# Keeping the sums of w_in from block 1 in HBM, in a retention and quick-GELU kernel

## The chip, the cores and the metric

The kernel runs on one core of a Trainium2 chip. The metric is device time in microseconds (us). Before the change, three runs gave a median of 659.03 us (656.14, 659.03 and 660.89).

The engines are named as in the profile: PE is TensorE's matrix multiply and PEld its weight load, DVE is VectorE, ACT is ScalarE, POOL is GpSimd, SP is SyncE. ACT, POOL and SP can each issue DMAs from a queue of their own; "ACTq" or "SPq" is such an instruction in that engine's stream.

## The reference

A recurrent retention layer over 4 batches, 8 heads, 768 steps and head size 64 gives x (3072 tokens by 512). Behind it stands a two-layer network with w_in (512 by 2048) and w_out (2048 by 512):

```python
state = gamma[None, :, None, None] * state + np.einsum('bhd,bhe->bhde', k[:, :, t], v[:, :, t])
y[:, :, t] = scale * np.einsum('bhd,bhde->bhe', q[:, :, t], state)
...
h = x @ w_in
g = h * (1.0 / (1.0 + np.exp(-1.702 * h)))
return (g @ w_out).astype(np.float32)
```

All is float32; the kernel is handed the two weight matrices as 64-bit numbers and narrows them itself.

## The kernel before

The 3072 tokens are worked through in six blocks of 512 (two halves of 256). Retention is done in steps of 64 positions; its step j is `step`, `attend`, `masked`, `by_state`, `output`, `aged` and `updated`. A block's *first product* is x @ w_in with the gate, its *second product* is g @ w_out.

**The sums.** From block 1 on, the first product is done with seven products of half-size matrices instead of eight. A 512 by 256 piece of w_in (two of the eight column groups p, so four pieces d = 0 to 3) is held as four quarters w0 to w3 in W1A. The seven products need four sums of them: w4 = w2 + w3, w5 = w4 - w0, w6 = w0 - w2, and w1 - w5. Block 0 needs no sums; its first product (`up0`, PE line 417) reads w0 to w3 as they are.

**Where the sums were made.** Twice:

- For block 1's first product (`seven`, PE line 492; sums in `seven_4`, `seven_6`, `seven_52`, `seven_w`, `seven_v`) into tiles of their own, one set for each d in the order 2, 0, 1, 3. Set 2 is made by DVE (lines 449, 453, 458, 459). In the other three, DVE makes w4, ACT writes a negated quarter (lines 465 and 474), and POOL issues a DMA from SBUF to SBUF that adds the other quarter to it (lines 467 and 475). The fourth sum, called w2, had a tile of its own, in the slot kT or tmp.
- Once more, for blocks 2 to 5, by POOL in `sums_w1` (lines 522 to 527), during block 1's second product: three sums into W1L, a view of the tile LATE, and the fourth in place over w2 in W1A.

LATE (48 rows of 128 numbers in each partition, 3 MB in all) has other uses too. Block 0 keeps gated results in it until its second product is over. From block 2 on, parts of it hold what `stream` and `derive` need for the second product. So in block 2, behind the first and the second `up`, SP stored LATE's two halves to the HBM tiles W1D[0] and W1D[1] (line 1003), and blocks 3 to 5 load them back (line 766 by ACT, line 999 by POOL).

**What sets the order.** Up to the end of block 1's first product, the order of the work is written out by hand as a list of words (lines 959 to 977); each word is a function that issues its instructions, and `pin` keeps each engine's order as written. `abs9` is ACT's first step of narrowing a piece of weights, `half9` and `rest9` are DVE's; `w9a` and `w9b` are SP's loads of the raw piece; `q7`, `v7` are loads for a retention step; `gate0.1.3` is ACT's gate for `up0.1.3`; `seven2.4` is the fifth of the seven products for d = 2. Behind the list PE still goes in program order; the other engines' instructions are placed by a scheduler where they are not kept in order. An engine works through its stream in order, so a DMA that waits on ACT holds what is behind it on ACT.

Between the products of `seven`, ACT copies the running sum out of PSUM (`p1`, `u` and `vv`, line 497) before PE may go on adding to that bank, one product later.

Before, the calls around the change in the loop over the blocks m were:

```python
pool.dma_start(LATE[:, 0:24], W1D[0])                                        # line 999, m > 2
tc.keep_in_program_order(sp.dma_start(W1D[n], LATE[:, 24 * n:24 * n + 24]))  # line 1003, m == 2, n < 2
if m == 1 and n % 8 == 3:
    sums_w1(n // 4)                                                          # line 1020
```

Of the kernel before, what the change touches and what calls it, by code (L numbers as in the profile page):

```python
# [9 lines left out]
F32 = mybir.dt.float32  # L10
U32 = mybir.dt.uint32
AF = mybir.ActivationFunctionType
ALU = mybir.AluOpType
P = 128
# [14 lines left out]
def kernel(  # L29
# [29 lines left out]
    pe, act, dve, pool, sp = nc.tensor, nc.scalar, nc.vector, nc.gpsimd, nc.sync  # L59
# [19 lines left out]
    one = ctx.enter_context(tc.tile_pool(name="one", bufs=1))  # L79
    two = ctx.enter_context(tc.tile_pool(name="two", bufs=2))  # L80
# [9 lines left out]
    W1A = const.tile([P, NP, 4, 2, P], F32, name="W1A")  # L90
    LATE = late.tile([P, 2 * NP * 3, P], F32, name="LATE")
    W1L = LATE.rearrange("p (n s c) f -> p n s c f", s=3, c=2)
    W1D = [dram.tile([P, NP * 3, P], F32, name=f"W1D{i}") for i in range(2)]
# [20 lines left out]
    def w1(p, s):  # L114

        return W1A[:, p, s] if s < 4 else W1L[:, p, s - 4]

    def w1s(p):

        return [W1A[:, p:p + 2, s] for s in range(4)] + [W1L[:, p:p + 2, s] for s in range(3)]  # L120

    ordered = [True]

    def pin(i):
        return tc.keep_in_program_order(i) if ordered[0] else i
# [142 lines left out]
    def decay(j):  # L268

        if j % NC == NC - 1:  # L270
            return
        KD[j] = home(j, "kd")
        x = QKV["kn", j]
        if j < NEW:

            for h in range(H):
                pin(act.activation(KD[j][:, h], x[:, h % HP * 2 + h // HP], AF.Copy, scale=cold[:, H + h:H + h + 1]))
        else:
            pin(pool.tensor_mul(KD[j].rearrange("p (i s) d -> p i s d", i=2), x.rearrange("p (i s) d -> p i s d", i=2),
                                cold[:, None, H:H + HP, None].to_broadcast([P, 2, HP, D])))  # L280
# [152 lines left out]
    SUM_X, SUM_W = {}, {}  # L433
# [20 lines left out]

    def seven_52(d):
        m = SUM_W[d]
        m.append(one.tile([P, 2, 2 * P], F32, name="w2", tag="kT"))
        pin(dve.tensor_sub(m[5], m[4], m[0]))
        pin(dve.tensor_sub(m[7], m[1], m[5]))

    def seven_w(d):

# [6 lines left out]
    def seven_v(d):  # L469

        m = SUM_W[d]
        m.append(one.tile([P, 2, 2 * P], F32, name="w2", tag="kT") if d == 1 else
                 two.tile([P, 2, 2 * P], F32, name="w2", tag="tmp", bufs=1))
        pin(act.activation(m[7], m[5], AF.Copy, scale=-1.0))
        pin(pool.dma_start(m[7], m[1], accum_op=ALU.add))

    SEVEN, GATES = {}, []

# [4 lines left out]
    def seven(d, k):  # L483
# [34 lines left out]
            pin(dve.tensor_add(a[2], acc, SEVEN["t"]))  # L518
        else:
            GATES.append(((a[3], a[3]), (a[2], a[2]), (a[1], acc)))  # L520

    def sums_w1(p):
        w = w1s(p)
        pool.tensor_add(w[4], w[2], w[3])
        pool.tensor_sub(w[6], w[0], w[2])
        pool.tensor_sub(w[5], w[4], w[0])
        pool.tensor_sub(w[2], w[1], w[5])

    def sums_x():
        tc.keep_in_program_order(pool.tensor_sub(X[:, 4], X[:, 2], X[:, 0]))  # L530
# [10 lines left out]
    def sums_w2_t3(p):  # L541
        dve.tensor_sub(W2[:, 6, p:p + 2, :], W2[:, 5, p:p + 2, :], W2[:, 0, p:p + 2, :])
# [92 lines left out]
    def inner_w2_t3(i):  # L635

        b11, b12, b21, b22 = w2q(ORDER[i][1])
        tc.keep_in_program_order(dve.tensor_sub(b12, b22, b12))
# [12 lines left out]
    def stream(i, engine=pool):  # L651

        c = LATE[:, i % 2 * 24:i % 2 * 24 + 12].rearrange("p (k d) e -> p k d e", k=3)
        engine.dma_start(c, W2D[i])  # L654
        return c
# [273 lines left out]
    works |= {"seven_x": seven_x, "seven_end": seven_end}  # L929
    for d in range(NP // 2):  # L930
        works |= {f"seven_{n}.{d}": lambda d=d, do=do: do(d)
                  for n, do in (("4", seven_4), ("6", seven_6), ("52", seven_52), ("w", seven_w), ("v", seven_v))}
        for n in range(7):
            works[f"seven{d}.{n}"] = lambda d=d, n=n: seven(d, n)
    for i in range(2 * NFF):
        works[f"w{i // 2}{'ab'[i % 2]}"] = lambda i=i: fetch(i)
    for name, i in [("0a", 0), ("0b", 1)] + [(str(p), 2 * p) for p in range(1, NFF)]:
        n = Narrow(i)
# [20 lines left out]
    for name in """  # L959
        k0 table q0 warm turn0 w0b rows warm k1 abs0b q1 turned0 step0 v0 w0a half0b mask k2 turn1 causal rest0b  # L960
        masked0 decay0 v1 decay1 abs0a half0a step-0 updated0 turned1 q2 step1 rowd whole w2b turn2 w2a x0 k3
        aged1 masked1 turned2 v2 rest0a abs2 q3 step-1 updated1 state1 decay2 aged2 step2 q4 x1 half2 decay3 w3b
        w3a up0.0.0 masked2 turn3 k4 step-2 v3 q5 rest2 k5 gate0.0.0 turned3 updated2 state2 step3 up0.0.2
        masked3 abs3 half3 x2 rest3 turn4 w1b step-3 aged3 gate0.0.2 turned4 state3 w1a w5b updated3 v5 decay4
        abs1 x3 turn5 half1 up0.0.3 turned5 up0.1.2 step4 aged4 w5a rest1 v4 gate0.0.3 decay5 w6a masked4
        gate0.1.2 abs5 w6b step5-4 half5 rest5 up0.0.1 updated4 abs6 state4 gate0.0.1 w4b
        up0.1.1 half6 aged5 w4a up0.0.5 rest6 masked5 up0.1.5 gate0.1.1 x4 gate0.0.5 abs4 step-5 w8b w8a
        half4 gate0.1.5 state5 updated5 anew q6 up0.1.6 x5 rest4 gate0.1.6 abs8 v6 decay6 aged6 up0.0.6 w7b w7a half8
        turn6 gate0.0.6 up0.1.0 abs7 seven_4.2 seven_6.2 half7 gate0.1.0 w9b w9a up0.1.4 q7 gate0.1.4 step6 masked6 rest7 up0.0.4 v7
        gate0.0.4 seven_52.2 turn7 up0.1.3 gate0.1.3 step7-6 seven_4.0 masked7 updated6 decay7 aged7 abs9 state6 x6 up0.0.7 rest8 seven_w.0 gate0.0.7  # L970
        w11a w11b step-7 state7 x7 seven_x half9 w10b w10a up0.1.7 gate0.1.7
        seven2.0 seven2.1 abs11 rest9 seven2.2 seven_v.0 w12a w12b seven2.3 half11 seven2.4 abs10 seven_4.1 seven_w.1
        seven2.5 rest11 seven2.6 w14b w14a seven0.0 seven0.1 half10 seven0.2 abs12 seven0.3 rest10 w13a w13b seven0.4
        seven_v.1 seven0.5 seven_4.3 half12 seven_w.3 seven0.6 seven1.0 abs14 seven1.1 rest12 w15a w15b seven1.2 seven1.3
        half14 seven1.4 abs13 seven_v.3 seven1.5 updated7 rest14 seven1.6 seven3.0 seven3.1 half13 seven3.2 abs15 seven3.3
        rest13 seven3.4 seven3.5 late_loads half15 rest15 seven3.6 seven_end
    """.split():
        works[name]()
    ordered[0] = False
    INNER = [(0, 19), (0, 22), (0, 26), (1, 2), (1, 12), (1, 15), (1, 18)]  # L980
    for m in range(NB):
        between = []
        if m == 0:
            between = [lambda: None, lambda: None, lambda: turn(2 * CB), lambda: step(2 * CB), lambda: None,
                       lambda: turn(2 * CB + 1)]
        elif m == 1:
            between = [lambda: (decay(2 * CB), load(2 * CB + 1, "v"))]
            for j in range(2 * CB + 1, 3 * CB + 1):
                between.append(lambda j=j: (step(j, j - 1), j < 3 * CB and turn(j + 1)))
        elif 1 < m < NB - 1:  # L990
            last = min((m + 2) * CB, NCH - 1)
            for j in range((m + 1) * CB + 1, last + 1):
                between.append(lambda j=j: (step(j, j - 1), j < last and turn(j + 1)))
            if last == NCH - 1:
                between.append(lambda: step(None, NCH - 1))
        if m > 1:
            ds = (0, 1, 2, 3) if m == 2 else (2, 3, 0, 1)
            if m > 2:
                pool.dma_start(LATE[:, 0:24], W1D[0])
            for n, d in enumerate(ds):  # L1000
                up(d, ds[n - 1] if n else None, ds[n + 1] if n < 3 else None)
                if m == 2 and n < 2:
                    tc.keep_in_program_order(sp.dma_start(W1D[n], LATE[:, 24 * n:24 * n + 24]))
                if n == 0 and m < NB - 1:
                    turn((m + 1) * CB + 1)
                if d == 0:
                    comps = {0: stream(0)}
                if n == 2:
                    comps[1] = stream(1)
                if m == 2:  # L1010
                    for i in range(2 * d, min(7, 2 * d + 2)):
                        inner_w2_t3(i)
        for n, unit in enumerate(down(m) if m < 2 else down49(m, comps)):
            unit()
            if m == 0 and n < NP and n % 2:
                sums_w2(n - 1)
            if m == 0 and NP <= n < 3 * NP // 2:
                sums_w2_t3(2 * (n - NP))
            if m == 1 and n % 8 == 3:
                sums_w1(n // 4)  # L1020
            if (m, n) in INNER:
                inner_w2(INNER.index((m, n)))
            if between and (n in (2, 5, 11, 16, 21) if m == 1 else n % 3 == (1 if m else 2)):
                between.pop(0)()
            if 0 < m < NB - 1 and n == (23 if m == 1 else 11):
                sums_x()
# [46 lines left out]
```

## Time and profile before

The profiled execution spans 659.4 us from its first to its last instruction; the profile gives no other time for it, and its span lies between the timed runs. PE's granted clock over the span was 0.995 of full speed.

| stage | us from the start | what happens |
|---|---|---|
| loading, first steps | 0 to 44 | PE busy 32.0 us, DMA engines full |
| block 0's first product, retention steps 4 to 7 | 44 to 103.3 | PE busy 58.1 us |
| block 1's first product with the sums | 103.3 to 151.7 | ACT busy 24.7 us |
| second products of blocks 0 and 1 | 151.7 to 259.5 | POOL busy 50.8 us |
| block 2 | 259.5 to about 364 | SP's two stores to W1D at 267.2 and 286.2 |
| blocks 3, 4, 5 | 364 to 659.4 | W1D loaded back three times |

Other rows that the change touches:

| what | number |
|---|---|
| DMA traffic in all | 89.77 MB |
| LATE<-W1D, 1536 KB each | by ACT's queue 3 times, 7.6 us to landing; by POOL's 3 times, 7.8 us |
| SP's two issues of W1D<-LATE | 0.40 and 0.60 us, 7.3 to 8.5 us to landing with all transfers of W1D |
| ACT's negations, L465 (6) and L474 (3) | about 0.62 us each |

A busy time is a sum over instructions; a gap on an engine matters only if PE, which is busy 97% of the span, ends up waiting for it. A wait is put down to what came last.

### The profile page before, as it was taken

What the parts mean: (1) busy time and instruction counts of PE and PEld (TensorE: products, weight loads), DVE (VectorE), ACT (ScalarE), POOL (GpSimd) and SP (SyncE); (2) the same over time, 40 slices, a digit from 0 to 9 for tenths busy, and PEclk for the clock granted to TensorE, in tenths of its full rate; (3) what the DMA queues carried; (4) which work ended last, traced back from release to release, by engine and by line L of the source; (5) the groups of instructions that cost most, each with busy time, mean ns of one, the idle gap of its engine ahead of it and who ended that gap; (6) DMA issues with size and microseconds to landing.
All of it is one profiled execution on the core that took longest, in us unless ns stands there. A gap on an engine that the chain in (4) does not pass through costs nothing.

```text
span 659.4 us, 15196 instructions
## 1 busy us (share of the span) xinstructions
PE 639.5 (97%) x6390; PEld 577.1 (88%) x6390; DVE 427.4 (65%) x599; ACT 165.2 (25%) x320; POOL 195.7 (30%) x222
## 2 busy tenths in 40 slices
PE   6789999999999999999999999999999999999997
PEld 3678888888788888889999888999888999888997
DVE  3699989999936963348883336984145984144855
ACT  4674334551000000333101323100333210233210
POOL 6400321210478218000727400535500335500000
PEclk9799999999999999999999999999999999999999
DMA  9996649763243456550577821486741244601142
GB/s 174 185 274 186 175 89 246 188 139 54 48 96 144 120 155 160 183 169 1 157 161 213 224 50 49 124 192 175 235 79 49 71 141 145 237 2 49 52 157 97
DMA packets 148149, 89.77 MB, mean 136 GB/s; under 512 B 131600, under 2 KB 134416, under 8 KB 147056
## 3 DMA queue, kind: packets, MB, share of 16 engines
q1 hardware_dynamic: 135856, 44.66, 30.2%
q0 software_dynamic: 9456, 38.16, 18.5%
q10 hardware_dynamic: 2768, 5.96, 2.6%
q8 instruction: 50, 0.82, 0.5%
q14 instruction: 19, 0.16, 0.1%
HBM read 71.32 MB, written 14.94 MB: 131 GB/s over the span
## 4 chain that ended last, share of the span: by engine, by line
PE 83%; DMA 8%; DVE 4%; SPq 2%; POOL 1%; issue 1%; ACT 0%; DVEq 0%; ACTq 0%; POOLq 0%
PE pq L679 22%; PE px L564 16%; PE pd L814 13%; PE pz L564 8%; PE ph L417 8%; PE ph L492 7%; PE py L564 4%; DMA W<-in_moe_w_in_dram 2%; PE pa L294 2%; DMA LATE<-W1D 1%; DMA G<-in_moe_w_in_dram 1%; PE py L317 1%; PE py L311 1%; PE pa L302 1%; DMA kn_in<-in_k_dram 1%; SPq L146 1%
## 5 line engine op out<-in xcount | busy, mean ns | idle before, releaser
L654 POOL DMA_DIRECT2D LATE<-W2D x28 | 15.5, 555 | 236.4 <-PE pq L679 125.0
L679 PE MATMUL pq<-W,G 128*128 128x128 f32 x672 | 80.2, 276 | 0.0
L679 PEld LDWEIGHTS pq<-W,G 128*128 128x128 f32 x672 | 77.6, 192 | 0.6
L564 PE MATMUL px<-X,LATE 128*128 128x256 f32 x256 | 60.7, 380 | 2.2 <-DMA LATE<-W1D 1.2
L564 PE MATMUL px<-X,W1A 128*128 128x256 f32 x256 | 60.5, 379 | 0.0
L679 PE MATMUL pq<-LATE 128*128 128x128 f32 x448 | 59.8, 276 | 0.0
L417 PE MATMUL ph<-X,W1A 128*128 128x256 f32 x256 | 57.4, 382 | 1.6 <-DVE X L352 1.1
L564 PEld LDWEIGHTS px<-X,LATE 128*128 128x128 f32 x256 | 48.5, 190 | 9.5 <-issue 1.5
L417 PEld LDWEIGHTS ph<-X,W1A 128*128 128x128 f32 x256 | 48.0, 190 | 8.5 <-DVE X L352 1.2
L679 PEld LDWEIGHTS pq<-LATE 128*128 128x128 f32 x448 | 54.5, 192 | 0.4
L564 PEld LDWEIGHTS px<-X,W1A 128*128 128x128 f32 x256 | 48.4, 190 | 6.5
L814 PE MATMUL pd<-W,G 128*128 128x256 f32 x224 | 49.6, 381 | 0.0
L814 PEld LDWEIGHTS pd<-W,G 128*128 128x128 f32 x224 | 42.2, 190 | 5.8
L599 DVE TENSOR_TENSOR G<-pz,vv 128x512 f32<-128x512 f32 x16 | 11.1, 692 | 49.3 <-ACT vv L579 49.3
L398 ACT ACTIVATE G<-G 128x512 f32<-128x512 f32 x48 | 29.8, 628 | 44.4 <-DVE G L607 22.2
L814 PE MATMUL pd<-W,LATE 128*128 128x256 f32 x160 | 35.8, 382 | 1.2 <-DVE LATE L548 1.2
L814 PEld LDWEIGHTS pd<-W,LATE 128*128 128x128 f32 x160 | 30.1, 190 | 6.2 <-DVE LATE L548 2.2
L701 ACT ACTIVATE o<-pq 128x512 f32<-128x512 f32 (+1 forms) x14 | 7.6, 544 | 90.8 <-PE pq L679 90.8
L564 PE MATMUL pz<-X,W1A 128*128 128x256 f32 x128 | 30.3, 379 | 0.0
L564 PE MATMUL py<-X,W1A 128*128 128x256 f32 x128 | 30.2, 379 | 0.0
L564 PE MATMUL pz<-X,LATE 128*128 128x256 f32 x128 | 30.2, 379 | 0.0
L679 PE MATMUL pq<-LATE,G 128*128 128x128 f32 x224 | 29.6, 275 | 0.0
(206 smaller groups left out, 1175.3 us busy)
## 6 DMA issues: line engine op xcount, KB each, us to landing
LATE<-W2D POOLq DMA_DIRECT2D x28, 768.0 KB, 5.0
W<-in_moe_w_in_dram SPq DMA_DIRECT2D x12, 512.0 KB, 4.8
W<-in_moe_w_out_dram SPq DMA_DIRECT2D x10, 512.0 KB, 5.0
out_dram<-o POOLq DMA_DIRECT2D x20, 256.0 KB, 3.8
q_sq<-in_q_dram SPq DMA_DIRECT2D x144, 32.0 KB, 2.5
k_sq<-in_k_dram SPq DMA_DIRECT2D x144, 32.0 KB, 2.2
v_in<-in_v_dram SPq DMA_DIRECT2D x72, 64.0 KB, 3.0
LATE<-W1D ACTq DMA_DIRECT2D x3, 1536.0 KB, 7.6
```

Source lines behind the costliest of these rows:

```text
L146: keep(engine.dma_start(*((to, at) if name == "v" else (to[:, n:H:2], at[:, n * HP:(n + 1) * HP]))))
L294: pe.matmul(pa[HALF[w], u, 0, s, :], kt[HALF[u], w, s, :], qt[HALF[u], w, s, :], start=True, stop=True)
L302: pe.matmul(pa[HALF[u], w, 1, s, :], kd[HALF[w], HP * u + s, :], vn[HALF[w], HP * u + s, :], start=True, stop=True)
L398: pin(act.activation(g, h[:, i], AF.Gelu_apprx_sigmoid))
L417: pe.matmul(h[:, ab], w, X[:, 2 * th + c // 2, c % 2, :], start=(ab == 0 and c == 0), stop=(c == 3), skip_group_check=True)
L492: pe.matmul(acc[:, u, :], w, x, start=(start and u == 0 and c == 0), stop=(stop and c == 1), skip_group_check=True)
L564: pe.matmul(acc[:, u, :], w1(2 * d + u, sw)[:, c, :], X[:, sx, c, :], start=(start and u == 0 and c == 0), stop=(stop and c == 1), skip_gr ...
L599: dve.tensor_add(a[3], z, v)
L654: engine.dma_start(c, W2D[i])
L679: pe.matmul(p0[:, j, :], a[:, d], w[:, d], start=(new and j == 0 and d == 0), stop=(d == NP // 2 - 1), skip_group_check=True)
L701: act.activation(to, y, AF.Copy)
L814: pe.matmul(p0[:, n, :], g1(m, p, sa)[:, n * P:(n + 1) * P], W2[:, sb, p, :], start=(new and p == 0 and n == 0), stop=(last and p == NP - ...
```

## The change

The sums made for block 1's first product are no longer thrown away.

- The fourth sum is written in place over w2 in W1A (by DVE in set 2, by ACT and POOL's adding DMA in the others) and has no tile of its own any more.
- The other three of a set are stored to W1D by three DMAs on ACT's queue (`seven_out`), for sets 0, 1 and 3 right behind `seven_v`, for set 2 behind `step7-6` in the list. Each store moves 256 KB in rows of 1 KB.
- POOL's `sums_w1` and the helper `w1s` are gone.
- At the start of block 1's second product ACT's queue loads LATE's two halves from W1D; SP's two stores in block 2 are gone.

```diff
     def seven_52(d):
         m = SUM_W[d]
-        m.append(one.tile([P, 2, 2 * P], F32, name="w2", tag="kT"))
+        m.append(m[2])
         pin(dve.tensor_sub(m[5], m[4], m[0]))
-        pin(dve.tensor_sub(m[7], m[1], m[5]))
+        pin(dve.tensor_sub(m[2], m[1], m[5]))
...
     def seven_v(d):
 
         m = SUM_W[d]
-        m.append(one.tile([P, 2, 2 * P], F32, name="w2", tag="kT") if d == 1 else
-                 two.tile([P, 2, 2 * P], F32, name="w2", tag="tmp", bufs=1))
-        pin(act.activation(m[7], m[5], AF.Copy, scale=-1.0))
-        pin(pool.dma_start(m[7], m[1], accum_op=ALU.add))
+        m.append(m[2])
+        pin(act.activation(m[2], m[5], AF.Copy, scale=-1.0))
+        pin(pool.dma_start(m[2], m[1], accum_op=ALU.add))
+        seven_out(d)
+
+    def seven_out(d):
+
+        to = W1D[d // 2].rearrange("p (n s c) f -> p n s (c f)", s=3, c=2)[:, d % 2 * 2:d % 2 * 2 + 2]
+        for n in range(3):
+            pin(act.dma_start(to[:, :, n], SUM_W[d][4 + n]))
...
-    def sums_w1(p):
-        w = w1s(p)
-        pool.tensor_add(w[4], w[2], w[3])
-        pool.tensor_sub(w[6], w[0], w[2])
-        pool.tensor_sub(w[5], w[4], w[0])
-        pool.tensor_sub(w[2], w[1], w[5])
...
-        gate0.0.4 seven_52.2 turn7 up0.1.3 gate0.1.3 step7-6 seven_4.0 masked7 updated6 decay7 aged7 abs9 state6 x6 up0.0.7 rest8 seven_w.0 gate0.0.7
+        gate0.0.4 seven_52.2 turn7 up0.1.3 gate0.1.3 step7-6 seven_out.2 seven_4.0 masked7 updated6 decay7 aged7 abs9 state6 x6 up0.0.7 rest8 seven_w.0 gate0.0.7
...
         elif m == 1:
+            for n in range(2):
+                act.dma_start(LATE[:, 24 * n:24 * n + 24], W1D[n])
             between = [lambda: (decay(2 * CB), load(2 * CB + 1, "v"))]
...
-                if m == 2 and n < 2:
-                    tc.keep_in_program_order(sp.dma_start(W1D[n], LATE[:, 24 * n:24 * n + 24]))
...
-            if m == 1 and n % 8 == 3:
-                sums_w1(n // 4)
```

More of the change, by code (lines that the diff above doesn't have):

```diff
@@ L116, in w1 @@
         return W1A[:, p, s] if s < 4 else W1L[:, p, s - 4]
-    def w1s(p):
-        return [W1A[:, p:p + 2, s] for s in range(4)] + [W1L[:, p:p + 2, s] for s in range(3)]
     ordered = [True]
@@ L931 @@
         works |= {f"seven_{n}.{d}": lambda d=d, do=do: do(d)
-                  for n, do in (("4", seven_4), ("6", seven_6), ("52", seven_52), ("w", seven_w), ("v", seven_v))}
+                  for n, do in (("out", seven_out), ("4", seven_4), ("6", seven_6), ("52", seven_52), ("w", seven_w), ("v", seven_v))}
         for n in range(7):
```

## The prediction

> **What bounds the kernel now.** I read the page's busy shares first, then PE's waits from 44 us to the end, then the busy time by stage, then single engines around the edits.
>
> ```profile
> PE 639.5 (97%) x6390; PEld 577.1 (88%) x6390; DVE 427.4 (65%) x599; ACT 165.2 (25%) x320; POOL 195.7 (30%) x222
> ```
>
> PE works 639.5 of 659.4 us. The 19.9 us without PE are 12.0 in the first 44 us (loading), 3.9 in the last 48 and little between. PE's waits from 44 us on (line, who was waited for, total us, times, longest):
>
> ```profile
> PE pd L814 <- DVE LATE L548: 1.2, 2, 0.9
> PE px L564 <- DMA LATE<-W1D: 1.2, 1, 1.2
> PE px L564 <- POOL X L532: 1.0, 1, 1.0
> PE pa L294 <- DVE G L323: 0.9, 1, 0.9
> PE ph L417 <- DVE W1A L227: 0.5, 1, 0.5
> ```
>
> Stages (window, length, busy us of PE, PEld, DVE, ACT, POOL, then clock, DMA share, GB/s):
>
> ```profile
> 103.30:151.70 48.40, 48.40 (x226) 42.61 (x225) 46.40 (x56) 24.66 (x41) 9.29 (x8) 1.00 0.73 183
> 165.00:180.00 15.00, 13.83 (x92) 11.07 (x90) 15.00 (x22) 0.00 (x0) 6.16 (x5) 1.00 0.28 53
> 180.00:213.00 33.00, 33.00 (x156) 28.79 (x156) 15.91 (x15) 1.79 (x3) 27.00 (x21) 1.00 0.37 112
> ```
>
> 103 to 152 is block 1's first product, where the sums are made: PE has no gap, DVE 2.0 us in 48.4. At 165 to 180 DVE is full and PE loses 1.2. At 180 to 213 POOL makes its second set, and PE has no gap. PE's idle time over all middle stages is 1.25 + 1.17 + 0.54 + 0.49 + 1.04 + 0.12 = 4.6 us. The change adds and removes no matmul and touches neither the first 44 us nor the tail. So 4.6 us (0.7%) is the most that it can give.
>
> **POOL's second set, removed.** Four sums, four times:
>
> ```profile
> L524 POOL TENSOR_TENSOR LATE<-W1A x4: 1257/1259/1712, 179.3 to 184.7; 128x512 f32<-128x512 f32 x4
> L527 POOL TENSOR_TENSOR W1A<-W1A,LATE x4: 1272/1598/1612, 200.4 to 209.7; 128x512 f32<-128x512 f32 x4
> ```
>
> With L525 and L526 the timeline's pieces add to 5.4 + 6.0 + 6.0 + 6.1 = 23.5 us of POOL. All of it lies beside a PE without a gap; behind it in POOL's queue stand an output store at 211.2 and block 2's decay (L279) at 214.3, and no PE wait names either. The sums' first reader is block 2 at 259.5. Gain: 0. DVE gets quicker beside an idle POOL, but there PE does not wait for DVE. Nothing moves into the 1.2 us at 165 to 180: the sums begin at 179.3.
>
> **The fourth sum in place.** Same instructions, other address. DVE's L459 (set 2) now has to wait for PE's last read of the old values, in up0.0.4. ACT's gate of that product runs at 89.03, L459 at 89.94: 0.9 us of cover. Behind L459 stand the transposes for step 7, then `masked7`, on which PE would wait; without the cover, up to 0.9 us. I take 0. ACT's L474 overwrites columns whose block-0 readers ended long before. Waits go by slices: L524 wrote its slice of LATE at 179.3 while PE read other slices until 202.3. The freed slots (kT, tmp) end no wait in the profile: 0.
>
> **Twelve stores on ACT, 256 KB each in 1 KB rows.** The trace has exactly this form in the last block (min/median/max ns):
>
> ```profile
> L712 ACTq DMA_DIRECT2D out_dram<-o x3: 379/384/397, 627.3 to 651.4; - x3
> ```
>
> So 3 x 0.384 = 1.15 us of ACT for a set. ACT around them (start, us, line, and idle before):
>
> ```profile
> 109.09 0.60 ACT L497 ACTIVATE u<-ph 128x512 f32<-128x512 f32 x1
> 109.57 0.64 ACT L398 ACTIVATE G<-G 128x512 f32<-128x512 f32 x1
> 110.09 0.64 ACT L474 ACTIVATE w<-w 128x512 f32<-128x512 f32 x1
> 112.01 0.60 ACT L497 ACTIVATE vv<-ph 128x512 f32<-128x512 f32 x1 [1.28 <-PE ph L492]
> ```
>
> - Set 2, behind a gate that ends at 93.15: abs9 and set 0's negations (L465) end at 96.4 instead of 95.25, and POOL's transfer that waits for them starts at 96.40 anyway, behind L364. 0.
> - Set 0, behind L474: 110.73 + 1.15 = 111.88, before `vv` at 112.01. 0; if an issue took SP's 0.6 us for a 64 KB load (L149), `vv` would be 0.5 late, within the 1.1 us that the next product (1.73) leaves beside `vv` (0.60).
> - Set 1: L474 ends at 125.27, then L465 at 127.5 instead of 126.3; `p` at 129.32 follows 3.0 us of idle ACT. 0.
> - Set 3: 138.43 + 1.15 = 139.6; `p` at 141.41. 0.
>
> Their data are ready: set 0's accumulating transfers are issued at 96.4 and 97.2 and land within 7.1 us, before 110.7; set 1's by 121.5, before 125.3; set 3's by 136.9, with the store due after 138.4.
>
> **DMA engines.** Price of a store: ACT's queue moved 5.96 MB in 2.6% of 659.4 = 17.1 us of all 16 engines, 0.75 us per 256 KB; a set 2.2 us, all 9.0. Room is short:
>
> ```profile
> 94.00:98.00 4.00, 4.00 (x50) 3.29 (x40) 3.93 (x6) 1.25 (x3) 3.59 (x4) 1.00 0.37 83
> 98.00:110.00 12.00, 12.00 (x145) 10.66 (x145) 11.04 (x15) 3.85 (x7) 0.61 (x1) 1.00 1.02 269
> 112.00:124.00 12.00, 12.00 (x57) 10.56 (x56) 11.61 (x15) 6.99 (x11) 2.33 (x3) 1.00 0.94 236
> ```
>
> Set 2 starts at 93.2 with 0.55 x 0.8 + 0.63 x 4 = 3.0 us free until 98, so it fits, but beside v for step 7:
>
> ```profile
> 92.40 3.36 SPq L149 DMA_DIRECT2D v_in<-in_v_dram  x4
> 98.06 0.69 PE L302 MATMUL pa<-v_in,G 64*64 64x64 f32 x32
> ```
>
> The last of the four starts near 95.1 and such a load took 3.0 us: 98.1, just when PE needs it. By 95.1 the stores have had about 1.1 us of free engines, 1.1 to 1.2 are left. The delay lies between 0 (other engines' gaps) and 2.2 (the whole set first); sharing with what is left gives up to 1.2, and I take half, **+0.6 us**. A rule of the Trainium skill speaks against the change: Trainium Kernel Development and Optimization, Key Constraints, says that DMAs from SP, ACT and POOL run on the same 16 engines and interleave, so that another queue saves only issue time. By it the stores are not free by being on ScalarE's queue; the share of 1.02 above, made by SP's and POOL's transfers together, is what this trace shows of it. By the rule, turn by turn, the end would be +1.2 (median 660.2); by the free share of the row alone, +0 (659.0).
>
> The next load, w11, is used the moment it lands (108.0), then `u` at 109.09, 0.6 us before PE would wait; it is issued at 101.87, after set 2 is through: 0, or 2.2 - 0.6 = 1.6 if it is not. Sets 0 and 1 meet covers of 5.0 us (w12 lands about 116.2, used 121.7) and 5 us (w13 131.7, 136.7); set 3's stores meet a share of 0.30 from 142 on. 0. The range keeps -0 and +3.8 us for this part.
>
> **LATE's two loads on ACT, SP's two stores gone.** The loads wait for PE's last reads of LATE at 202.7; behind them on ACT stands `p` at 209.68. They need 0.33 us each to issue and land 7.6 us later (the same transfer in later blocks), together under 16: by 219 for 259.5. 40 us of cover: 0; were it gone, up to 15 us at block 2's start. SP loses two issues of 0.5 us and 3 MB at 267 and 286, where PE had no gap: 0.
>
> **Sum.** 659.4 + 0.6 = 660.0 in the profiled execution's terms. Its span is 0.4 above the runs' median of 659.03, so 659.6.
>
> **The rivals.**
> 1. *Slower: a set's stores wait for one another.* They write interleaved rows of one HBM tile. If each has to land (4.8 us, L712's median) before the next is issued, ACT stands about 10 us instead of 1.15. Late would be `vv` of d = 0 (end 121.4 for a product due at 113.7: 7.7), `p` of d = 1 (137.0 for 131.0: 6.0), of d = 3 (149.0 for 143.1: 5.9) and 0.7 behind set 2: +20.3, 680. For it: no such tile is in the trace. Against: the last outputs, interleaved rows of one tensor, are issued at 654.7 and 655.5 though the first lands after 1.6 us.
> 2. *Slower: the engines overflow.* If a store costs 1.5 us or more instead of 0.75, set 2 needs 4.5 us with 3.0 free; v7 comes 3 us late, w11 2.4 too late after its cover, and DVE, with no room until 180, gives some 1.5 on: +7, 666. From 1.5 us a store it decides. Against: the same form in the last block moved with other traffic at 239 to 398 GB/s.
> 3. *A little faster.* Waits on L548, W1D and L532, 3.4 us, vanish through other timing: 655.6. None is named by the change.
> 4. *It does not do what it says.* A load of LATE placed ahead of block 0's copies on ACT would hold `vv` at 195.88 until PE is done; but PE needs `vv` before, so that order can't stand.
>
> **Chances.** Three runs spread over 4.8 us, 0.7%; 1% is what can be told. Forecast 0.80 (656 to 663; 0.01 beyond each bound), overflow 0.08, stores in turn 0.05, a little faster 0.07 (0.03 beyond 1% with a lucky median). Faster 0.04, slower 0.01 + 0.08 + 0.05 = 0.14, the same 0.82. The range goes from rival 3 to the upper bound of the unknown costs with the spread: 655.5 to 664.5; rivals 1 and 2 lie outside.
>
> **What would show it.** Right: no L524 to L527 on POOL; twelve ACT issues near 0.38 us at 93, 111, 126 and 139; PE's one new wait on v_in at 98, under 1.2 us; 40 us between LATE's landing and its use. Wrong: a new PE wait on ACT's `vv` or `p` in 110 to 150 (rival 1), on DVE or DMA there (rival 2), or a middle stage that becomes shorter by more than its idle time.

## The result and the profile after

Six timed executions of the changed kernel have a median of 667.95 us, six of the kernel before 659.96 us: ratio 1.0121 with a 95% interval from 1.0092 to 1.0151. The change costs 8.0 us, and the forecast (659.6, range to 664.5) was wrong. The profiled execution spans 666.4 us, 7.0 more than before. Line numbers of the changed kernel are four or five lower than those of before (L548 became L543, L302 became L298). In the profile's lines `W1A` holds the pieces of w_in and `w` their sums; `kn_in`, `v_in`, `q_sq` and `k_sq` are loads for a retention step.

The page's busy line after:

```profile
PE 639.7 (96%) x6390; PEld 576.6 (87%) x6390; DVE 419.8 (63%) x599; ACT 165.8 (25%) x320; POOL 172.5 (26%) x206
```

POOL works 23.2 us less and PE just as long as before: the 7 us are idle time of PE. PE's waits from 44 us on, after (line, who was waited for, total us, times, longest):

```profile
PE pa L298 <- POOL G L275: 2.2, 1, 2.2
PE pa L290 <- DVE kT L254: 1.5, 1, 1.5
PE pd L809 <- DVE LATE L543: 1.2, 2, 0.9
PE ph L413 <- DVE W1A L223: 0.9, 1, 0.9
PE pa L290 <- DVE G L319: 0.9, 1, 0.9
PE pd L809 <- DVE G L543: 0.6, 1, 0.6
PE py L307 <- DVE X L348: 0.6, 1, 0.6
PE ph L494 <- ACT u L499: 0.6, 1, 0.6
PE py L313 <- issue: 0.5, 1, 0.5
PE pa L298 <- DMA v_in<-in_v_dram: 0.5, 1, 0.5
```

Three of these, on LATE from L543, on L223 and on L319, were there before (as L548, L227 and L323). The new ones fall into two places. To find them I laid both traces side by side by the first matmul of each stage (us; the first row is the first matmul behind the loading, two earlier `up0` stand within it):

| stage | before | after | difference |
|---|---|---|---|
| end of the loading, start of the third `up0` | 44.34 | 44.91 | +0.57 |
| from there to block 1's first product (retention step 7 is in it) | 58.83 | 61.90 | +3.07 |
| block 1's first product | 48.35 | 49.18 | +0.83 |
| block 0's second product | 51.00 | 51.02 | +0.02 |
| block 1's second product | 56.77 | 60.90 | +4.13 |
| block 2 to the last matmul's end | 396.84 | 394.93 | -1.91 |

The rest of the 7.0 is +0.3 in the tail. The stages of after that answer to those of the prediction (columns as there):

```profile
98.00:110.00 12.00, 9.38 (x131) 7.97 (x130) 8.35 (x11) 1.86 (x4) 5.06 (x4) 1.00 0.66 130
...
106.80:156.00 49.20, 48.63 (x226) 42.49 (x225) 46.34 (x57) 24.62 (x40) 9.45 (x8) 1.00 0.85 233
...
207.00:267.90 60.90, 58.08 (x705) 49.41 (x704) 35.07 (x53) 1.79 (x3) 15.84 (x17) 1.00 0.58 174
```

At 98 to 110 PE now lacks 2.6 us and the DMA engines are *less* busy than before (0.66 for 1.02): something kept transfers from being issued. In block 1's second product PE lacks 2.8 us, with POOL busy 15.8 us of 60.9 and DVE little more than half; the other 1.3 us of the 4.1 the profile doesn't show as idle.

**First place: step 7.** SP's queue waits of after, between 80 and 112 us, and its timeline there (start, us, line, count):

```profile
SPq L145 <- DMA W1D<-w: 4.2, 2, 3.5
```

```profile
90.34 6.07 SPq L145 DMA_DIRECT2D kn_in<-in_k_dram  x4
96.51 3.20 SPq L145 DMA_DIRECT2D v_in<-in_v_dram  x4
```

SP stands 4.2 us for *ACT's* stores, though no load of its own reads or writes W1D or the sums. Its four kn loads take 6.07 us to issue; before, 2.58:

```profile
89.72 2.58 SPq L149 DMA_DIRECT2D kn_in<-in_k_dram  x4
```

The list of waits of the compiled program says why (position on the queue, line, transfer, what it waits for):

```
SP   94 L145 kn_in  [waits DMAHW7, Pool]      ACT  79 L477 W1D<-w  [waits DMAHW2, DVE]
SP   95 L145 kn_in  [waits DMAHW0]            ACT  80 L477 W1D<-w  [waits DMAHW4, DVE]
SP   96 L145 kn_in  [waits DMAHW1]            ACT  81 L477 W1D<-w  [waits DMAHW6]
SP   97 L145 kn_in  [waits DMAHW2]
SP   98 L145 v_in   [waits DMAHW3, PE]
SP   99 L145 v_in   [waits DMAHW4]
SP  100 L145 v_in   [waits DMAHW5]
SP  101 L145 v_in   [waits DMAHW6]
```

A completion semaphore counts up when a transfer has landed. SP's and ACT's transfers take turns on eight of them, and one can be issued only when the last on its semaphore has landed. In the records of both traces SP and ACT use one set of eight semaphores, POOL's transfers another eight. Before, ACT had no transfer here and SP's loads waited for SP's own earlier ones. Now the three stores sit on the semaphores that the fourth kn load and the second and fourth v loads take next. POOL's decay of step 7 needs the kn loads, and PE needs the decay. POOL's decay before, then POOL's and PE's timelines after (last bracket: idle before, and what ended it):

```profile
94.41 1.04 POOL L279 TENSOR_TENSOR G<-kn_in,cold 128x512 f32<-128x512 f32 x1 [13.87 <-DMA kn_in<-in_k_dram]
```

```profile
98.91 1.90 POOL L275 TENSOR_TENSOR G<-kn_in,cold 128x512 f32<-128x512 f32 x1 [17.81 <-DMA kn_in<-in_k_dram]
```

```profile
100.86 0.40 PE L298 MATMUL pa<-v_in,G 64*64 64x64 f32 x6 [2.17 <-POOL G L275]
101.71 0.62 PE L298 MATMUL pa<-v_in,G 64*64 64x64 f32 x25 [0.45 <-DMA v_in<-in_v_dram]
```

The decay starts at 98.91 instead of 94.41. What is behind on SP, w11, is late too, and `u` with it (0.6).

**Second place: block 1's second product.** ACT's queue and SP's, after:

```profile
203.80 3.79 ACTq L983 DMA_DIRECT2D LATE<-W1D  x2
```

```profile
204.36 13.75 SPq L627 DMA_DIRECT2D W2D<-X  x2
```

The first of LATE's two loads starts half a microsecond ahead of a store of 768 KB that SP makes anyway, the second 2.9 us behind it: DVE makes inner sums of w_out in X (L626), SP stores them to W2D, and the next sums go into the same X. So DVE waits for the landing, and its queue holds all that is behind. The chain of waits has that store in it, and DVE's timeline has the two waits:

```profile
204.36 11.23 DMA W2D<-X
...
217.79 5.43 DMA W2D<-X
```

```profile
215.62 0.69 DVE L626 TENSOR_TENSOR X<-W 128x512 f32<-128x512 f32 x1 [7.71 <-DMA W2D<-X]
...
223.25 0.69 DVE L626 TENSOR_TENSOR X<-W 128x512 f32<-128x512 f32 x1 [5.48 <-DMA W2D<-X]
```

The engines' share (second last column) between 205 and 215, first after, then before:

```profile
205.00:210.00 5.00, 5.00 (x25) 4.41 (x24) 0.69 (x1) 0.00 (x0) 0.73 (x1) 1.00 0.98 304
210.00:215.00 5.00, 5.00 (x24) 4.38 (x24) 0.00 (x0) 0.60 (x1) 0.00 (x0) 1.00 1.01 424
```

```profile
205.00:210.00 5.00, 5.00 (x25) 4.41 (x24) 4.09 (x3) 0.32 (x1) 4.84 (x5) 1.00 0.05 20
```

In the chain the second store lands after 11.2 us, and DVE's longest wait for one is 7.7 us; before, it was 4.6. DVE's waits for W2D between 200 and 245 us, before and after:

```profile
DVE X L631 <- DMA W2D<-X: 10.3, 3, 4.6
```

```profile
DVE X L626 <- DMA W2D<-X: 13.2, 2, 7.7
```

They come later, too: the sums of g behind them (L541 to L543) run at 229.6 to 238.8, before at 220.6 to 229.6. PE waits for these and for the retention step beside them. The Trainium skill's DMA: Bandwidth & Descriptors, section Queues, rings and completion order, says that each DMA engine takes turns between its queues packet by packet; a store slowed by another queue's loads agrees with it.

### The profile page after: what moved, and what is told of

It is laid out like the page before. It is cut to its first block, busy times and chain, and to the rows that moved or that the text cites. A ratio compares the mean times of both kernels' runs of the same rounds, so it can differ in the third digit from the quotient of the medians.

```text
span 666.4 us, 15205 instructions
## 1 busy us (share of the span) xinstructions
PE 639.7 (96%) x6390; PEld 576.6 (87%) x6390; DVE 419.8 (63%) x599; ACT 165.8 (25%) x320; POOL 172.5 (26%) x206
## 3 DMA queue, kind: packets, MB, share of 16 engines
q10 hardware_dynamic: 6320, 12.26, 5.3%
## 4 chain that ended last, share of the span: by engine, by line
PE 76%; DMA 11%; DVE 9%; SPq 2%; issue 1%; ACT 1%; POOL 0%; DVEq 0%; ACTq 0%; POOLq 0%
PE pq L674 27%; PE px L559 17%; PE pz L559 8%; PE ph L494 6%; PE pd L809 6%; PE py L559 4%; PE ph L413 3%; DMA W2D<-X 3%; DMA W<-in_moe_w_in_dram 2%; DMA G<-in_moe_w_in_dram 1%; SPq L159 1%; PE pa L290 1%; DMA W<-in_moe_w_out_dram 1%; PE py L313 1%; PE py L307 1%
## 5 line engine op out<-in xcount | busy, mean ns | idle before, releaser
L674 PE MATMUL pq<-W,LATE 128*128 128x128 f32 x224 | 29.6, 275 | 0.0
```

Source lines behind the costliest of these rows:

```text
L674: pe.matmul(p0[:, j, :], a[:, d], w[:, d], start=(new and j == 0 and d == 0), stop=(d == NP // 2 - 1), skip_group_check=True)
```

## The experiments

The theory: **A**, ACT's set 2 holds up SP's loads through shared semaphores; **B**, LATE's early loads slow the W2D stores on which DVE stands. The rivals: the stores' bytes crowd out v and kn (my own forecast's mechanism, larger than I took it); ACT's issue time; the queue that LATE's loads sit on. Stage lengths below are those of the table; ratios are to the kernel before, with 95% intervals.

**Set 2's stores on another queue.** Same place in the list, same bytes, POOL instead of ACT:

```diff
-            pin(act.dma_start(to[:, :, n], SUM_W[d][4 + n]))
+            pin((pool if d == 2 else act).dma_start(to[:, :, n], SUM_W[d][4 + n]))
```

> The changed kernel, with set 2's three stores issued by POOL's queue instead of ACT's; same bytes, same place in the list. Theory (shared completion semaphores): in the list of waits of the changed program the fourth kn load and two of the v loads of step 7 each reuse the completion semaphore of one of ACT's three stores, so SP stands until the store has landed. POOL's stores take none of these eight semaphores: SP's four kn loads are issued in 2.6 us again instead of 6.1, PE's waits at step 7 (2.2 on POOL, 0.5 on v_in, 0.5 issue) go, `u` too: about 3.6 us of the 8.0 come back, ratio to the kernel before near 1.0065. Rival (the DMA engines' bandwidth at 94 to 96 us): the bytes are the same, so decay7 and v7 stay late: ratio 1.010 to 1.013.

1.0037 [1.0013, 1.0060]: 5.5 us of the 8.0 came back, more than the 3.6 expected. SP's timeline:

```profile
90.86 2.63 SPq L145 DMA_DIRECT2D kn_in<-in_k_dram  x4
```

Stage 44 to block 1's first product is back at 58.83 us, the wait on `u` is gone, and SP waits no more for W1D. The bytes are unchanged, so it isn't they. Block 1's second product still takes 59.07, 2.3 us more than before: B is left. It took 60.90 in the changed kernel, so 1.8 us of what came back lie there, where the edit changes nothing; A doesn't explain them, since the run with LATE's loads by ACT, below, has 58.90 there with A in place.

**The waits without the bytes.** The kernel before, with three stores of one number per partition (0.5 KB) at set 2's place on ACT's queue; nothing else of the change:

```diff
+            pin(act.dma_start(to[:, 0, n, 0:1], SUM_W[d][4 + n][:, 0, 0:1]))
```

> The kernel before, with three stores added on ACT at set 2's place, of one number a partition (0.5 KB each) instead of 256 KB; what they write is written again later and is not used. Theory (shared completion semaphores): such a store still lands only some 2 us after its issue at 93.1, the fourth kn load has to wait for it and is issued near 95 instead of 91.7: PE loses 1.5 to 3 us at step 7, ratio 1.002 to 1.005, with PE's wait on POOL's decay in the profile. Rival (bandwidth): 1.5 KB cost nothing, no new wait, ratio 1.000.

1.0058 [1.0031, 1.0086]. SP's queue waits and timeline:

```profile
SPq L149 <- DMA W1D<-w: 1.9, 1, 1.9
```

```profile
91.69 4.48 SPq L149 DMA_DIRECT2D kn_in<-in_k_dram  x4
```

Three stores of 0.5 KB hold SP for 1.9 us. The stage grows by 2.2 us, `seven` by 1.0. But the sign that was expected, PE's wait on POOL's decay, is missing: the decay runs at 98.13 to 99.58, late but in time for PE at 99.92. 1.1 of the 2.2 is PE's wait at 94.2 for transposes of k_sq, whose loads were issued before the stores, and 0.3 is a wait on v. So this run shows SP's wait without the bytes, but hardly its price in PE's time; why the ratio is above the 1.002 to 1.005 expected stays open. (Block 0's second product took 49.17 us here, 1.8 less than before; the last section shows this in other kernels, without such stores.)

**Set 2's stores on ACT, later in the list.** `seven_out.2` moved from behind `step7-6` to behind `seven2.1`:

> The changed kernel with set 2's three stores still on ACT and of 256 KB, but some 14 us later in the list (behind the second of the seven products for d = 2), where the semaphores that they take come round to other transfers than step 7's. Theory (shared semaphores, by place and not by queue): SP issues step 7's loads without a break, PE's 3 us at step 7 go as with POOL; LATE's loads stay where they are: 1.0037 to 1.007. If stores on ACT's queue hold up SP's queue wherever they stand, the loads of w11 to w13 are late, ACT's copies and DVE with them, and little is won: 1.010 or more.

1.0083 [1.0058, 1.0108], a little above what was expected. SP's kn loads are back at 2.58 us, and step 7's loss is gone but for the same k_sq wait (1.26 of +1.33). The waits only changed sides. ACT's timeline and PE's waits:

```profile
106.12 4.86 ACTq L477 DMA_DIRECT2D W1D<-w  x3
```

```profile
PE ph L494 <- ACT u L499: 1.5, 1, 1.5
```

Now ACT stands for SP's loads, `u` is late behind it, and block 1's first product takes 50.10 us. B is untouched (59.32).

**LATE's loads later, two attempts.** The first took them out of the head of block 1's second product and put them behind its seventh step, by POOL and, as a control of the queue, by ACT:

```diff
+            if (m, n) == (1, 6):
+                for i in range(2):
+                    pool.dma_start(LATE[:, 24 * i:24 * i + 24], W1D[i])
```

> The changed kernel, with LATE's two loads moved from the start of block 1's second product to behind its seventh unit (some 12 us later, when the fourth W2D store has been issued), and issued by POOL. Theory (the loads take the DMA engines from the W2D store issued 0.6 us behind them, which lands after 11.2 instead of 3.9 us; DVE stands on it and brings block 1's sums of g late): DVE's wait on W2D falls from 19.5 to about 11 us, PE's gap of 4.2 us between 207 and 268 goes, ratio near 1.006. Rival (DVE and POOL run in another order because POOL's 23.5 us are gone): the gap stays, ratio 1.012.

> As the run with LATE's loads later, but issued by ACT. If only the DMA engines' time matters, the same as by POOL (ratio near 1.006). If the eight completion semaphores that ACT and SP share matter here too, SP's loads of q, k and v that come round to the semaphores of LATE's loads wait for 7.7 us, and some of the gain is lost: ratio 1.007 to 1.012.

1.0064 [1.0041, 1.0087] and 1.0121 [1.0079, 1.0163]. Neither moved the loads: the scheduler put the unpinned loads where they had been. So the 1.0064, though it was expected, is no success of the expectation. POOL's timeline:

```profile
202.49 0.57 POOL L1014 DMA_DIRECT2D LATE<-W1D  x1 [0.82 <-issue]
...
207.10 0.57 POOL L1014 DMA_DIRECT2D LATE<-W1D  x1
```

The run by ACT (issued at 202.96) is in effect the changed kernel again, and has its ratio. On POOL's queue the two came 4.6 us apart, and block 1's second product took 57.63 instead of 58.91. So with POOL issuing them B was smaller; whether by the queue or by the time between the two loads, the runs don't separate. Step 7 lost 3.1 us there, as in the changed kernel; 4.6 in the run by ACT, where the clock fell as in the next run.

The second attempt pinned them behind the last W2D store:

```diff
+            if (m, n) == (1, 18):
+                for i in range(2):
+                    tc.keep_in_program_order(pool.dma_start(LATE[:, 24 * i:24 * i + 24], W1D[i]))
```

> The changed kernel, with LATE's two loads on POOL and this time held in order behind the last W2D store (some 50 us later; in the two earlier runs the scheduler issued them near 203 us as before). Theory (LATE's loads and the W2D stores share the DMA engines; DVE stands on the stores): W2D's second store lands in 4 to 5 us instead of 11, DVE's waits on W2D fall from 19.5 to 11 us or less, PE's gap between 207 and the start of block 2 (4.1 us) goes; step 7 stays 3 us late: ratio 1.005 to 1.007. Rival (that gap comes of another order on DVE and POOL): the gap stays, 1.011 to 1.013. If the loads now come too late, PE waits for LATE at block 2's start.

1.0128 [1.0094, 1.0162]; the expectation missed. B itself is gone: the stage takes 56.77 us, as before. POOL's sums are missing here too, so another order of work on DVE and POOL was not its cause. Two other things cost time. Step 7 lost 4.8 us in this execution instead of 3.1; within it PE was granted half the clock for 3.4 us, worth 1.7 us (the last three columns are the granted clock, the DMA engines' share and GB/s; this run, then after):

```profile
102.00:105.40 3.40, 3.40 (x60) 2.92 (x52) 1.82 (x3) 0.00 (x0) 1.51 (x2) 0.50 0.91 164
```

```profile
102.00:105.40 3.40, 3.40 (x96) 3.10 (x89) 1.98 (x3) 0.00 (x0) 1.97 (x2) 1.00 0.78 142
```

And PE is idle for 2.0 us at block 2's start, until 269.71, with nobody named; DVE and ACT show what ran just before:

```profile
PE px L559 <- issue: 2.0, 1, 2.0
```

```profile
268.20 0.69 DVE L785 TENSOR_TENSOR o<-pd,t 128x512 f32<-128x512 f32 x1 [8.87 <-DMA out_dram<-o]
```

```profile
269.01 0.60 ACT L568 ACTIVATE p<-px 128x512 f32<-128x512 f32 x1 [11.00 <-DVE o L785]
```

It is not LATE that is late: its halves, issued at 254.2 and 254.8, land after 8.1 and 12.6 us, the second at 267.4, before PE's gap begins. DVE's last output sum `o` waits 8.9 us for an output store to land, one that POOL issued at 261.2 beside LATE's loads and that took 6.9 us; ACT's copy `p` of px comes behind that sum, and PE goes on in px when the copy is done. Read so, it is B again with another store: before, this sum ran at 259.54 and waited for PE alone. No run tried this by itself.

**Both mends.** Set 2's stores on POOL, and LATE's loads as just above:

> Both mends together: set 2's stores by POOL, LATE's loads by POOL behind the last W2D store. If the two causes are all, and add up: 1.0121 less 0.006 for step 7 and u, less 0.006 for LATE's loads, that is 1.000, less up to 0.003 for the waits that became shorter in blocks 3 to 5: 0.997 to 1.001, with no PE wait over 1.3 us after the first 44 us. If a third cause remains, 1.003 or more.

1.0046 [1.0022, 1.0070]; expected was 0.997 to 1.001. Both stages are back (59.39, 56.77), and block 2's start loses 1.8 us in the same way: the output store takes 6.8 us, DVE's last `o` runs at 264.60, PE goes on at 266.10. (A wait of 0.4 on LATE is in block 3.) With the first half by POOL behind the sixth W2D store instead:

> Set 2's stores by POOL; LATE's first half by POOL behind the sixth W2D store (near 243 us), its second half behind the last. If lateness at block 2 was the rest of 1.0046: that wait goes, ratio 0.999 to 1.003. The sixth store is the one that DVE waits for least (0.5 us), but if it lands 7 us later beside the load, DVE's step 12 is late and PE loses 1 to 3 us before block 2: 1.003 to 1.006.

1.0022 [1.0005, 1.0040]; 1.6 us on issue remain at block 2, until 265.60, though LATE's halves have landed by 253.6 and 262.1: DVE's last `o` runs at 264.10. With the first half by SP behind the fourth W2D store, and the second by POOL behind the last:

```diff
+            if m == 1 and n in (2, 18):
+                i = n // 18
+                tc.keep_in_program_order((sp, pool)[i].dma_start(LATE[:, 24 * i:24 * i + 24], W1D[i]))
```

> Set 2's stores by POOL; LATE's first half loaded by SP behind the fourth W2D store (near 217 us), its second half by POOL behind the last W2D store (near 250). With both halves on POOL behind the last store the run gave 1.0046, and PE waited 2.0 us in all at block 2's start. If that lateness was the rest, and 1.5 MB at 217 hurt nobody: block 1's second product stays at 56.8 us, that wait goes, ratio 0.999 to 1.003. If SP's loads of k, q and v behind it become late, PE shows waits at the steps between 225 and 250, 1.003 to 1.008.

0.9997 [0.9981, 1.0013], 660.36 us. SP's timeline, with the load behind the stores instead of ahead of them, and PE's waits:

```profile
199.39 11.38 SPq L627 DMA_DIRECT2D W2D<-X  x3
210.86 0.39 SPq L1016 DMA_DIRECT2D LATE<-W1D  x1
```

```profile
PE pd L809 <- DVE LATE L543: 1.2, 2, 0.9
PE ph L413 <- DVE W1A L223: 0.9, 1, 0.9
PE pa L290 <- DVE G L319: 0.9, 1, 0.9
PE px L559 <- DMA LATE<-W1D: 0.5, 1, 0.5
```

Here the output store took 4.1 us, DVE's last `o` runs at 260.37 and block 2's start has no gap; so the expectation's range was hit, but LATE's lateness, its reason, was not what cost time. All stages have the lengths of before within 0.4 us, but for block 2 onward (395.74, which is 1.1 shorter); the loading was 0.8 us shorter in this trace, whose granted clock was 1.000. A and B together account for the loss. And with both away, the change brings nothing that can be measured: POOL's 23 us were free, as they lay beside a PE without a gap.

**SP's two stores in block 2 put back**, to see whether their absence gave the -1.9 us of blocks 2 to 5:

> The changed kernel with SP's two stores of LATE to W1D in block 2 put back (they write what is there already). In the changed kernel blocks 2 to 5 take 1.9 us less than before (393.9 against 395.8 us from block 2's first matmul to the last). If SP's missing stores are the reason, the 1.9 us come back: ratio 1.015. If it is only where the transfers happen to fall, 1.012 stays.

1.0103 [1.0062, 1.0144]; blocks 2 to 5 took 395.99 us, between after (394.93) and before (396.84). The ratio doesn't differ from that of the changed kernel, so the run decides nothing.

**The kernel before, unchanged**, as a control:

> The kernel before itself, as a control: 1.000 within 0.003 if programs are compared fairly. Its second profile shows whether the loading stage (first matmul of block 0's product at 44.3 us) and PE's 1.2 us of waits on L548 differ from one execution to the next by themselves; 1 to 2 us either way are expected.

1.0007 [0.9987, 1.0027]. Its start was 0.64 us later than in the first profile, and the stage of step 7 0.59 us longer: differences of this size between two traces mean nothing by themselves. The +0.57 at the start of after is one.

## Why the prediction was wrong, step by step

- **What bounds the kernel: right but for a slip.** The last 48 us lack 3.3 us of PE and not 3.9 (12.0 + 4.6 + 3.3 = 19.9); nothing rests on it.
- **POOL's second set, gain 0: right.** In the version with both causes away, 23 us less of POOL give 0.9997. DVE did get quicker beside an idle POOL (L626's pair of sums 1.42 us, before 2.14 and 3.32), and PE got nothing of it, as priced.
- **The fourth sum in place, 0: right.** No wait names it.
- **Twelve stores, 3 x 0.384 us on ACT: right as issue time** (0.37 to 0.52 us each), and so is the refusal of rival 1: set 2's three were issued at 93.1, 93.6 and 94.1, landings were 2.2 to 5.0 us. No wait of PE comes from their issue time.
- **DMA engines, "+0.6" at step 7: this step failed.** The place was right; mechanism and size weren't. I priced the stores' bytes against v's landing, with 3.0 us of free engines. The stage lost 3.1 us: PE waited 2.2 for the *decay* behind the kn loads and 0.5 for v, because SP could not *issue*. I had listed what was queued behind the stores on ACT, and the queue that they were moved to, but not what SP's loads would wait for; the bytes on POOL's queue cost step 7 nothing. Rival 2 named a late v7 and w11 for the same wrong reason, and its own test, 1.5 us of engine time a store, was not what decided: the price of 0.75 us per 256 KB held on ACT's queue (12.26 MB in 5.3% of 666.4 us).
- **w11, "0, or 1.6 if it is not": inside those ends.** `seven` lost 0.8 us, of which 0.6 on `u`. I took 0 because I let w11 be issued on time.
- **LATE's two loads, "40 us of cover: 0": this step failed too, and it is the larger term, +4.1 us.** The cover is real for who reads LATE: PE's waits from 44 us on name LATE's loads nowhere in the lines above. The question left out was who else needs the engines at 204 us, and who stands on that: the W2D store lay in the trace of before, with DVE waiting 10.3 us on such landings. Free engines (a share of 0.05) looked like room; they were room that a wait depended on. How much is lost varies with the run: where ACT issues the first load at 200 to 204 us, five programs with the same W2D stores, the stage lost 2.1 to 4.1 us. What sets it between these ends was not found.
- **SP's stores gone, 0: not settled.** Blocks 2 to 5 took 1.9 us less in one trace; putting the stores back didn't decide it. A second trace of the kernel before was 0.7 us shorter there than the first. Of rival 3's waits, those on LATE (1.2) and on POOL's X (1.0), both in blocks 3 to 5, are not in after's list; in other kernels they are there with 0 to 1.4 us. They come and go, as the rival had it, and are no effect of the change that a run shows.
- **The chances.** I gave 0.82 to within 1% because the two steps above had one mechanism each (bytes, readers). The skill's rule on shared engines, taken turn by turn as in the prediction, would have added another 0.6 us: also too little, since it too is about engines at work and not about an issue that waits.

## What to carry to other kernels

When a transfer is moved to another engine's queue, look up in the compiled program which completion semaphore it takes and whose next transfer takes it again: separate queues may still wait for one another's landings, even for half a kilobyte. When a load is moved to where "its data are needed only much later", price it at the place where it *starts*: find the transfers that run there, and the in-order engines that reuse a buffer only after those have landed. Pin a transfer whose time matters, and read in the trace when it was issued before concluding anything from its place in the program.

## What was unexpected in the hardware

When DVE and POOL both make 128x512 sums, one of the two is slowed, and which one differs between runs. Block 0's second product took either about 51.0 us or 49.17 us, in kernels that issue the same sums of g there. The version at 0.9997 and the first one with both mends are such a pair: they differ only in LATE's loads, some 30 us later. DVE's and POOL's timelines of the former (50.97 us):

```profile
171.92 1.76 DVE L541 TENSOR_TENSOR X<-LATE,X 128x512 f32<-128x512 f32 x1
...
174.80 1.75 DVE L541 TENSOR_TENSOR g<-LATE,g 128x512 f32<-128x512 f32 x1
```

```profile
171.55 1.58 POOL L547 TENSOR_TENSOR LATE<-LATE 128x512 f32<-128x512 f32 x1 [3.29 <-DVE LATE L543]
174.42 1.58 POOL L547 TENSOR_TENSOR LATE<-LATE 128x512 f32<-128x512 f32 x1 [1.29 <-DVE LATE L543]
```

Here DVE's sums that meet POOL's take 1.75 us, others 0.68, and POOL's take 1.58. In the other (49.17 us) POOL came to its first sum at 175.23, again just ahead of DVE's third L541, and it is POOL that stands: its four sums take 9.33 us, the first alone 5.19.

```profile
175.23 9.33 POOL L547 TENSOR_TENSOR LATE<-LATE 128x512 f32<-128x512 f32 x4 [3.28 <-DVE LATE L543]
```

There each of DVE's L541 sums took 0.69 us beside it, and PE's 1.2 us of waits on L543 did not appear. Four of the profiled kernels fell this way; DVE's order of work at this place is the same in all. What tips it was not tried; a difference of 1.8 us in that stage is no evidence of what an edit elsewhere did.
